# Decode attention and gated MLP on one core: two ring slots exchanged, x moved to the sync queue behind the q weights, the last W_down read cut into 5, 3 and 1 rows

## Chip, cores and metric

One core of a Trainium2 chip. The metric is the device time of one execution in microseconds (us), lower is better. Runs of one kernel mostly lie within 1 us of their median, single ones up to 1.6 us off. The profiled span is about 1.8 us shorter than the device time of the same run (381.1 for 382.86): it runs from the program's first instruction to its last.

Names used below, as in the profile of the kernel before: PE runs the matmuls (1629; PEld is the loading of their weights, 1629 too), DVE, ACT and POOL run the other operations (157, 95 and 38 instructions), and SP issues all loads but x. The loads run as packets on 16 DMA engines; 4224 of the 6390 packet records, with 87% of the bytes, are of 32 KB. A load's landing is the last update of its semaphore in the trace (16 updates for a 4 MB tile, 5 for x). The granted clock is the share of full speed that the profile gives for PE, in the mean 0.864 before.

## The reference

A batch of 4 tokens goes through a pre-norm attention over the last 4096 positions of a cache, then a pre-norm ReGLU MLP:

```python
# x: 4 x 1 x 576; K and V cache: 4 x 16 x 16384 x 128; W = 4096; 32 q heads on 16 kv heads
q = (layernorm(x) @ wq).reshape(...)                    # wq 576 x 4096
k, v = k_cache[:, :, -4096:], v_cache[:, :, -4096:]     # each kv head serves 2 q heads
o = softmax(q @ k.T * 128 ** -0.5) @ v
h = x + o @ wo                                          # wo 4096 x 576
g = layernorm(h) @ W_gate                               # 576 x 4608, W_up the same
out = h + (relu(g) * (layernorm(h) @ W_up)) @ W_down    # 4608 x 576
```

Nearly all of it is reading: 159.6 MB, of which K and V are 134 MB in 32 tiles of 4 MB (K0 to K15, V0 to V15).

## The kernel before

All large loads are issued from SP, one after the other. K and V tiles and the q weights go through a ring of four 4 MB slots; a load into a slot waits, on SP, until the last reader of the slot is done, and everything behind it in SP's program waits with it: K3, and K4 behind it, waited 36.2 us there for K0's matmuls.

```python
def add_kv(kind, g):                 # next ring slot; its earlier owner must be finished
    s = ring_slot()
    place((kind, g), off, TILE, ("QK", g, 1) if kind == "K" else ("PV", g), ...)
...
add_kv("K", 0)                                            # slot 3
s = ring_slot(); place(("wq", 0), ..., "QMM", ...)        # slot 0: first 512 rows of wq
P.dma("sync", ("L", "wq", 1), ... last_rows(A_wq) ...)    # last 64 rows of wq, outside the ring
for g in range(1, NTILE):                                 # K1 slot 1, K2 slot 2, K3 slot 3, K4 slot 0,
    add_kv("K", g)                                        # V0 slot 1, K5 slot 2, V1 slot 3, K6 slot 0 ...
    if g >= 4:
        add_kv("V", g - 4)
...                                                       # then wo, W_gate, W_up
for j in range(4):                                        # W_down, 4 chunks of 9 rows per partition
    for r0, r1 in ((0, 9),) if j < 3 else ((0, 6), (6, 9)):
        place(("wd", j, r0), ...)
```

x (4.5 KB) was issued from ACT. In DVE's program the norm of x stands ahead of K0's transposes, and q_keep, which K0's matmuls need, stands behind them. The traces show them in that order: K0 had landed at 13.29 us before, but the transposes started behind the norm, at 14.59, and q_keep as they ended, at 29.25:

```python
P.dma("scalar", ("L", "x"), ... x_bf ...)
dve("bn0"), dve("bn1"), ...      # norm of x, 3.4 us to its transposed copy xnT
pe_x(); dve_x()                  # xnT
turn_k(0, 0); turn_k(0, 1)       # DVE: K0's two transposes, 7.4 us each; they do not read x
pe_q()                           # PE: q = xn @ wq ("QMM"); K3's or K4's slot is free after it
act_q(); dve_q()                 # q_keep
put_q(0); put_q(1)               # ACT: q into the matmuls' weights; K0's matmuls ("QK", 0) wait for it
```

## Time and profile before

| | before |
|---|---|
| device time, median of the first 3 runs | 381.62 us |
| data read | 159.6 MB, mean 419 GB/s over the span |
| packets in flight from 3.0 to 372.8 us (packet records) | 16 for 92% of the time, under 14 for less than 0.1 us in all |
| one 4 MB tile, landing to landing | 9.7 us |
| last W_down piece lands / last matmul ends | 377.55 / 378.41 us |

The page of the profile before: the busy share of the 16 DMA engines and their throughput in 40 equal slices of 9.5 us, and the queue that SP issues on with its share of the engines' span.

```profile
DMA  8999999999999999999999999999999999999993
GB/s 331 440 423 421 406 440 437 433 428 427 420 439 440 424 433 426 433 430 435 433 430 427 435 430 423 435 433 433 430 428 433 427 439 430 423 435 427 419 414 123
...
q1 hardware_dynamic: 6352, 159.59, 97.7%
```

The reader sees a kernel bound by its loads from the second slice to the last but one.

The timeline of the kernel before, DVE, ACT and PE in the first 46 us, six of its rows. Columns: start, duration, engine and line, operation, what it writes and reads, count, and in brackets the idle time ahead of it and what ended that.

```profile
11.19 0.80 DVE L354 BATCH_NORM_STATS2 sb_bn<-sb_x_bf 4x6 f32<-4x288 bf16 x2
14.59 14.69 DVE L432 STREAM_TRANSPOSE sb_arena<-sb_arena 128x4096 f32<-128x4096 f32 x2
23.01 3.60 PE L388 MATMUL psb<-sb_arena,sb_xnT 128*32 128x512 bf16 x32 [8.88 <-DMA sb_arena<-in_A_wq_dram]
29.25 0.68 DVE L409 CAST sb_q_keep<-psb 32x512 bf16<-32x512 f32 x1
29.96 2.53 ACT L418 COPY sb_arena<-sb_q_keep 32x128 bf16<-32x128 bf16 x8 [1.37 <-DVE sb_q_keep L409]
31.35 15.18 PE L450 MATMUL psb<-sb_arena 128*128 128x512 bf16 x47 [2.14 <-ACT sb_arena L418]
```

K0's two transposes take 14.7 us and end at 29.28; K0's matmuls start 2 us after that. The q weights landed before: the first 512 rows at 23.0, the last 64 at 24.2. The first norm instruction at 11.19 stands on DVE behind one that waited 7.2 us for a constant that POOL makes; x had been there since 2.4.

The timeline of SP of the kernel before, from K1 to V2: when each load was issued. The row of four holds K1 to K4; K3 is its third, issued at 40.09. Then come V0, K5, V1, K6, V2, K7, V3.

```profile
2.51 38.77 SPq L246 DMA_DIRECT2D sb_arena<-in_A_k_cache_dram  x4
53.90 0.54 SPq L246 DMA_DIRECT2D sb_arena<-in_A_v_cache_dram  x1
64.27 0.53 SPq L246 DMA_DIRECT2D sb_arena<-in_A_k_cache_dram  x1
74.64 0.54 SPq L246 DMA_DIRECT2D sb_arena<-in_A_v_cache_dram  x1
88.36 0.54 SPq L246 DMA_DIRECT2D sb_arena<-in_A_k_cache_dram  x1
97.43 0.54 SPq L246 DMA_DIRECT2D sb_arena<-in_A_v_cache_dram  x1
```

Each issue came before the stream had used up what was ahead of it. From 53 to 79 us the loads took 19 to 20 us to land, half of it spent queueing behind another tile (three issues of the kernel before, view of one line):

```profile
DMA to landing us min/median/max: 19.0/19.7/20.3
```

That queue is the margin. Taken from the first packet of a load (1.3 us after its issue) to the end of the packets ahead of it, it is 1 to 3 us at K3 (issued 40.09, K2's packets end at 42.6 to 44.5), 6 to 7 us at V0, K5 and V1, and only about 2 us at K6, on the engine that is done first.

### The profile page before, as it was taken

To read this page: it belongs to the slowest core of one execution; us is meant where nothing else is said; L and a number is where in the kernel's file an instruction comes from. 1 tells how busy PE (TensorE), PEld (TensorE's weight loads), DVE (VectorE), ACT (ScalarE), POOL (GpSimd) and SP (SyncE) were. 2 spreads that over 40 slices of the span, in tenths; PEclk is the share of its full clock that TensorE was granted. 3 is DMA by queue.
4 is the path that set the end of the run, shared out by engine and by line. 5 is a ranking of instruction groups with operands and counts; after the bars stand their busy time and mean duration, and the time that the engine had idled before them with its cause. 6 is when DMAs were issued, how large, how long until landed. Compare 5 with 4: busy or idle time off the path is not lost.

```text
span 381.1 us, 3671 instructions
## 1 busy us (share of the span) xinstructions
PE 278.0 (73%) x1629; PEld 92.8 (24%) x1629; DVE 223.2 (59%) x157; ACT 37.5 (10%) x95; POOL 16.3 (4%) x38
## 2 busy tenths in 40 slices
PE   0057999989959892979996939899969537036544
PEld 0013223322222221222221212222212213015322
DVE  0796799979383917965828279756464455002210
ACT  1112000015000006000000051000000340000100
POOL 8800000000000000000000000000000000000000
PEclk9998999989978897798997887989989956756687
DMA  8999999999999999999999999999999999999993
GB/s 331 440 423 421 406 440 437 433 428 427 420 439 440 424 433 426 433 430 435 433 430 427 435 430 423 435 433 433 430 428 433 427 439 430 423 435 427 419 414 123
DMA packets 6390, 159.81 MB, mean 419 GB/s; under 512 B 740, under 2 KB 744, under 8 KB 1384
## 3 DMA queue, kind: packets, MB, share of 16 engines
q1 hardware_dynamic: 6352, 159.59, 97.7%
q8 instruction: 12, 0.20, 0.2%
q14 instruction: 2, 0.02, 0.0%
q10 hardware_dynamic: 24, 0.01, 0.0%
HBM read 159.58 MB, written 0.00 MB: 419 GB/s over the span
## 4 chain that ended last, share of the span: by engine, by line
PE 44%; DMA 34%; DVE 15%; POOL 2%; ACT 2%; issue 1%; SPq 0%; POOLq 0%
PE psb L450 38%; DMA sb_arena<-in_A_k_cache_dram 19%; DVE sb_arena L432 11%; DMA sb_arena<-in_B_W_down_dram 9%; DMA sb_arena<-in_A_v_cache_dram 7%; PE psb L497 5%; POOL sb_arena L303 2%; ACT sb_pp L475 2%; DVE sb_o_sel L509 1%; DVE sb_o_tmp L505 1%; DVE sb_pp L484 1%; PE psb L534 0%; ACT sb_arena L418 0%; SPq L286 0%; PE psb L469 0%
## 5 line engine op out<-in xcount | busy, mean ns | idle before, releaser
L450 PE MATMUL psb<-sb_arena 128*128 128x512 bf16 x512 | 209.1, 578 | 10.5 <-DVE sb_arena L432 8.2
L432 DVE STREAM_TRANSPOSE sb_arena<-sb_arena 128x4096 f32<-128x4096 f32 x32 | 156.1, 4901 | 48.5 <-DMA sb_arena<-in_A_k_cache_dram 48.4
L450 PEld LDWEIGHTS psb<-sb_arena 128*128 128x128 bf16 x512 | 56.8, 114 | 153.6 <-issue 130.3
L497 PE MATMUL psb<-sb_arena,sb_pp 128*32 128x512 bf16 x512 | 35.9, 431 | 23.0 <-DMA sb_arena<-in_A_v_cache_dram 16.5
L475 ACT ACTIVATE sb_pp<-psb,sb_stat 128x512 bf16<-128x512 f32 x32 | 24.9, 847 | 247.8 <-DVE sb_stat L470 247.8
L505 DVE TENSOR_TENSOR sb_o_tmp<-psb,sb_qm 128x512 f32<-128x512 f32 x16 | 10.8, 676 | 27.9 <-PE psb L497 27.9
L497 PEld LDWEIGHTS psb<-sb_arena,sb_pp 128*32 128x32 bf16 x512 | 13.6, 106 | 47.9 <-issue 22.7
L457 DVE TENSOR_REDUCE sb_stat<-psb 128x1 f32<-128x1024 f32 x4 | 4.8, 1211 | 24.2 <-PE psb L450 24.2
L484 DVE STREAM_TRANSPOSE sb_pp<-sb_pp 128x2048 bf16<-128x2048 bf16 x8 | 18.0, 2278 | 1.4 <-ACT sb_pp L475 1.4
L509 DVE TENSOR_REDUCE sb_o_sel<-sb_o_tmp 128x128 f32<-128x512 f32 x16 | 16.6, 1037 | 0.6
L534 PE MATMUL psb<-sb_o_sel,sb_selw 128*32 128x32 f32 x128 | 2.4, 232 | 16.3 <-DVE sb_o_sel L509 16.3
L668 PE MATMUL psb<-sb_arena,sb_hnT 128*32 128x384 bf16 x120 | 7.9, 437 | 6.6 <-DMA sb_arena<-in_B_W_up_dram 4.5
L375 PE MATMUL psb<-sb_ident_b,sb_xn_bf 4*128 4x4 bf16 x4 | 0.3, 172 | 13.7 <-DVE sb_xnd_bf L364 13.7
L388 PE MATMUL psb<-sb_arena,sb_xnT 128*32 128x512 bf16 x32 | 3.6, 631 | 8.9 <-DMA sb_arena<-in_A_wq_dram 8.9
L675 DVE TENSOR_TENSOR sb_pp<-psb,sb_pp 128x384 bf16<-128x384 f32 x3 | 1.5, 551 | 12.6 <-PE psb L668 12.6
L517 PE MATMUL psb<-sb_stat,sb_sameh 128*128 128x1 f32 x8 | 1.8, 292 | 9.1 <-DVE sb_stat L515 9.1
L303 POOL MEMSET sb_arena<- 128x8192 f32 x1 | 6.9, 6925 | 0.0
L475 ACT ACTIVATION_READ_ACCUMULATOR sb_pp<-psb,sb_stat 128x1 f32 x32 | 6.6, 208 | 0.0
L668 PEld LDWEIGHTS psb<-sb_arena,sb_hnT 128*32 128x32 bf16 x120 | 4.2, 124 | 9.7 <-DMA sb_arena<-in_B_W_up_dram 4.8
L534 PEld LDWEIGHTS psb<-sb_o_sel,sb_selw 128*32 128x32 f32 x128 | 1.9, 142 | 17.4 <-DVE sb_o_sel L509 17.4
L701 PE MATMUL psb<-sb_arena,sb_pp 128*32 128x144 bf16 x144 | 3.8, 250 | 3.0 <-DMA sb_arena<-in_B_W_down_dram 2.5
L418 ACT COPY sb_arena<-sb_q_keep 32x128 bf16<-32x128 bf16 x16 | 4.8, 303 | 1.5 <-DVE sb_q_keep L409 1.4
(123 smaller groups left out, 71.9 us busy)
## 6 DMA issues: line engine op xcount, KB each, us to landing
sb_arena<-in_A_k_cache_dram SPq DMA_DIRECT2D x16, 4096.0 KB, 18.9
sb_arena<-in_A_v_cache_dram SPq DMA_DIRECT2D x16, 4096.0 KB, 24.2
sb_arena<-in_A_wo_dram SPq DMA_DIRECT2D x1, 4608.0 KB, 16.0
sb_arena<-in_B_W_gate_dram SPq DMA_DIRECT2D x1, 4608.0 KB, 30.9
sb_arena<-in_B_W_up_dram SPq DMA_DIRECT2D x1, 4608.0 KB, 42.3
sb_arena<-in_A_wq_dram SPq DMA_DIRECT2D x1, 4096.0 KB, 21.5
sb_arena<-in_B_W_down_dram SPq DMA_DIRECT2D x3, 1296.0 KB, 31.1
sb_arena<-in_B_W_down_dram SPq DMA_DIRECT2D x1, 864.0 KB, 32.7
```

The lines of the kernel that those rows point to most:

```text
L303: pool("c_qW", lambda e: e.memset(arena[:, 0:2 * QWW].bitcast(FP32), 0.0))
L418: act(("QW", b), lambda e, i=i: e.copy(out=bass.AP(tensor=arena, offset=32 * i * AW + b % 2 * QWW + 32 * i, ap=[[AW, 32], [128, 4], [514, ...
L432: dve(("TRA", g, w), lambda e: e.transpose(out=dst, in_=src), [("L", "K", g)] if w == 0 else [])
L450: pe(("QK", g, w), lambda e, off=off, steps=steps, wo_=wo_, qd=qd, first=first, last=a == cb == 3: e.matmul(bank[SB[b % 2] + w], lhsT=aren ...
L457: dve(("MAX", b), lambda e: e.tensor_reduce(out=stat[:, b, 0:1], in_=s_ps, axis=AX.X, op=ALU.max, negate=True), [("QK", 4 * b + 3, 1)])
L475: act(("EXP", b, w), lambda e, w=w, a=a: e.activation(out=bass.AP(tensor=pp, offset=4096 + a // 2 * 2048 + w * 1024 + a % 2, ap=[[8192, 12 ...
L484: dve(("PTR", b, w), lambda e: e.transpose(out=dst, in_=src), [("EXP", b, w), ("PV", 4 * b - 1) if b else "QMM"])
L497: pe(("PV", g), lambda e, j=j, tq=tq, k=k: e.matmul(o_ps[32 * j:32 * j + 32, :], lhsT=pT[:, qd * 1024 + tq * 32:][:, 0:32], rhs=v[:, tq * ...
L505: dve(("OS", g), lambda e: e.tensor_tensor(out=o_tmp[:, :].rearrange("p (t d) -> p t d", t=4), in0=o_ps.rearrange("p (t d) -> p t d", t=4) ...
L509: dve(("OSEL", g), lambda e: e.tensor_reduce(out=o_sel[:, qd, :], in_=o_tmp[:, :].rearrange("p (t d) -> p d t", t=4), axis=AX.X, op=ALU.ad ...
L534: pe(("OT", b), lambda e, q=q, qd=qd: e.matmul(ot_ps[32 * qd:32 * qd + 32, 0:32], lhsT=selw[:, qd, 32 * q:32 * q + 32], rhs=o_sel[:, qd, 3 ...
L668: pe(("GU", g, c // 4), lambda e, g=g, m=m, j=j, lo=lo, c=c: e.matmul(bank[3 * g + m][32 * j:32 * j + 32, 0:384], lhsT=hnT[:, c if c < 4 e ...
```

## The change

Three edits, each aimed at one wait: K3 may be loaded as soon as the q weights are used; x gives up its queue of its own (q10 in the trace before, its four packets start at 1.85 to 2.03 us) and goes in line on SP; and fewer matmuls (4 instead of 12) are left when the last piece of W_down lands.

```diff
+        first = ring[0]
+        ring[0] = first + 1
         add_kv("K", 0)
+        ring[0] = first
         s = ring_slot()
 ...
         P.dma("sync", ("L", "wq", 1), ... last_rows(A_wq) ...)
+        P.dma("sync", ("L", "x"), ... x_bf ...)
+        ring[0] = first + 2
         for g in range(1, NTILE):
 ...
-            for r0, r1 in ((0, 9),) if j < 3 else ((0, 6), (6, 9)):
+            for r0, r1 in ((0, 9),) if j < 3 else ((0, 5), (5, 8), (8, 9)):
 ...
-        P.dma("scalar", ("L", "x"), ... x_bf ...)
 ...
-                    if n == 0 and (r == 0 or (j == 3 and r == 6)):
+                    if n == 0 and (r == 0 or (j == 3 and r in (5, 8))):
```

More of the change, by code (lines that the diff above doesn't have):

```diff
@@ L260, in bass_sequential_preLN__sliding_block_cached__glu_gated_reglu__decode_kernel @@
         P.dma("sync", ("L", "wq", 1), lambda e: e.dma_start(out=pT[:, 0:2048], in_=last_rows(A_wq)), "d_wq1")
+        P.dma("sync", ("L", "x"), lambda e: e.dma_start(out=x_bf[:, :], in_=A_x.rearrange("b s d -> (b s) d")), "d_x")
+        ring[0] = first + 2
         for g in range(1, NTILE):
@@ L351, in bass_sequential_preLN__sliding_block_cached__glu_gated_reglu__decode_kernel @@
         act("warm_sqrt", lambda e: e.activation(out=warm[:, 0:1], in_=eps_c[:, :], func=ACT.Sqrt), ["c_eps"])
-        P.dma("scalar", ("L", "x"), lambda e: e.dma_start(out=x_bf[:, :], in_=A_x.rearrange("b s d -> (b s) d")), "d_x")
         for hf in range(2):
```

## The prediction

> **What bounds it now.** The load stream. The DMA row of the 40 slices is 9 from slice 2 to 39; queue q1 takes 97.7% of 16 engines' span. In the packet records 14 to 16 packets are in flight from 3.0 to 372.8 us. A 4 MB tile takes 9.7 us (landings 54.8, 64.5, 74.2 us). The last W_down piece lands at 377.55, the last matmul ends at 378.45.
>
> **Slot exchange.** K3 reuses the slot of K0 or wq. Before, it waited for K0's matmuls and was issued at 40.09 us, while K2's packets ended at 42.6 to 44.5: no engine ran dry. After, K3 waits for the q matmuls (about 32 us) and K4 for K0's. Gain: none; it only widens a margin.
>
> **x move.** Today x rides on the ACT queue: its four packets run at 1.9 us, its last semaphore update is at 2.4. [...] So x behind K0, wq and wq's last rows lands when those do, about 24.2 us. The norm chain now starts at 11.19, held by a constant from POOL, so it starts 13 us later. DVE is in order and K0's transposes (2 x 7.42 us) stand behind it: they end at 42.3, not 29.3. The q copies add 2.1: K0's matmuls start at 44.4 (31.35 before), end at 53.1 (40.09).
>
> **How much is critical.** I step the early ring forward with the trace's durations (QK: K0 8.7, K1 13.8, K2 and K3 10.4 us; issue to first packet 1.2 to 1.4):
> - K4 issued 53.1, K3's packets end 52.7 to 54.4: gap 0 to 1.6 us
> - V0 issued 67.0, K4's end 64.0: gap about 4
> - K5 77.3, V1 87.7: gaps about 0.7
> - K6: K4's matmuls end at 99.0 (88.36 before); gap 1.7
> - V2 needs PV0, after a PE stall on K5's first transpose; a clock dip to 0.5, as after the stall at 80 us today, would cost 1.7 us: issued 109 to 111, gap 0.4 to 2
>
> After that PE needs about 16 us per K and V pair and DMA 19.4: DMA is saturated again, but lost stream time is never regained. V2's packets end at 120 to 122 us; before 111.0 on the fastest engine, 112.6 on the slowest. The slowest sets the end: loss 7.4 to 9.2 us.
>
> **Tail.** Matmuls behind the last landing fall from 12 to 4, about 20 ns each, and the 3-row piece lands only 0.34 us earlier (estimate, from 430 GB/s). Gain 0.2 to 0.4 us; the added small DMA costs about 0.1.
>
> **Predicted:** 381.6 + 8.5 - 0.3 = 389.8 us, range 386.8 to 392.3. Faster by over 2%: 1%; within 2%: 39%; slower by over 2%: 60%.
>
> **What would show it.** The first norm instruction near 24.2 us instead of 11.2; K0's matmuls near 44.4. K3's issue near 32, K4's near 53. GB/s below 400 in slices 6 to 11, then as before, shifted. PE from 44 to 95 us almost solid. Last landing to last matmul 0.6 us instead of 0.9.
>
> **What would make it wrong.** x landing well before the q weights: then neutral, about 381.3. A different clock in the early stage (each 3.4 us dip moves it 1.7). The slowest engine's lag (3.3 us at the end of W_down) shrinking after the gaps, worth 1 to 2 us. Wider gaps if K4 or K5 stall more.

The landing near 24.2 us is the author's estimate, and the trace of the kernel before supports it: SP's loads landed in the order of their issue (K0 13.29, wq 22.96, wq's last rows 24.24, K1 33.96).

Its other figures of the hardware, as the traces have them: first packets 1.41 us after issue at K0, 1.32 and 1.31 at K4 and V0 after the change; clock dips to 0.5 from 31.29 to 34.70 and from 82.49 to 85.90 us before, 3.41 us each, half of which is the 1.7; W_down's matmuls 18 to 21 ns each (72 in 1.31 us, 36 in 0.75 us, before); the added piece under 0.1 us (e4).

## The result, and the profile after

The changed kernel takes 392.38 us (391.6 to 392.64, 4 runs) against 381.69 us (4 runs) before. The ratio is 1.0275 (95% interval 1.0255 to 1.0294): slower by over 2%. Ratios here are the mean time of one kernel's runs over that of the other's of the same rounds, so not quite the ratio of the medians quoted.

The page of the profile after, the same two rows of slices (of 9.75 us):

```profile
DMA  7999986999999999999999999999999999999994
GB/s 323 430 431 434 435 316 269 397 410 375 377 414 429 434 435 429 431 434 430 429 434 430 437 429 430 430 429 430 430 432 434 430 430 434 419 443 416 438 402 179
```

The loss sits in slices 6 to 12, about 49 to 117 us. Afterwards the stream runs at 430 GB/s as before, only later.

The chain of waits that ended last, followed in order of time, of the kernel after. Columns: start, duration, what the time went to.

```profile
2.51 21.79 DMA sb_x_bf<-in_A_x_dram
24.30 0.02 issue
24.33 0.82 DVE sb_bn L358 x2
...
27.68 6.29 DVE sb_arena L436
33.97 0.90 issue
34.87 7.40 DVE sb_arena L436
42.27 0.52 DVE sb_q_keep L413
...
44.21 49.21 PE psb L454 x140
...
96.05 4.37 DVE sb_arena L436
100.46 7.06 PE psb L454 x16
107.52 1.84 PE psb L501 x32
109.36 7.01 PE psb L454 x16
116.38 0.02 issue
116.39 16.53 DMA sb_arena<-in_A_k_cache_dram
```

This is the whole story in one column. x takes 21.8 us from issue to landing (4.5 KB!), then the norm runs, then K0's transposes, then PE is busy without a break for 49 us, and only at 116.4 does the chain go back to a load. In the chain of the kernel before, PE's first long stretch ended at 64.3, and a load (K5) came next.

The timeline of SP after, from x on. The row of four is K1 to K4; K3 was issued at 32.19 and K4 at 53.72, then V0, K5, V1, K6, V2.

```profile
2.51 0.64 SPq L264 DMA_DIRECT2D sb_x_bf<-in_A_x_dram  x1
3.19 51.06 SPq L246 DMA_DIRECT2D sb_arena<-in_A_k_cache_dram  x4
67.53 0.54 SPq L246 DMA_DIRECT2D sb_arena<-in_A_v_cache_dram  x1
77.90 0.53 SPq L246 DMA_DIRECT2D sb_arena<-in_A_k_cache_dram  x1
88.27 0.54 SPq L246 DMA_DIRECT2D sb_arena<-in_A_v_cache_dram  x1
99.44 0.54 SPq L246 DMA_DIRECT2D sb_arena<-in_A_k_cache_dram  x1
109.41 0.53 SPq L246 DMA_DIRECT2D sb_arena<-in_A_v_cache_dram  x1
```

V0, K5 and V1 are issued 13.6 us later than before, more than the 6 to 7 us of margin. K6 and V2 are 11 and 12 us later. The three issues from 53 to 79 us (K4, V0, K5) of the kernel after:

```profile
DMA to landing us min/median/max: 12.3/12.3/12.4
```

They no longer queue behind a whole tile. In the packet records the 16 engines stand idle for 2.4 us on average before K4, 3.7 before V0 and 0.1 before K5, whose first packets start just as V0's last ones end. A tile lands 12.3 us after its issue, but the next is issued 10.4 to 13.8 us after it (53.72, 67.53, 77.90, 88.27). The successive landings of K4, V0, K5, V1, K6, V2 and K7 come 11.7, 13.8, 10.4, 11.7, 10.6, 9.9 and 10.3 us after the one before, together 10.7 us more than seven times 9.7.

The packet records of this stage say what these microseconds are. From 43 to 124 us the engines stood idle for 7.6 us on average, and the 32 KB packets took 3.2 us per engine more than 1.21 us each would have; in e6, which lost nothing (see the experiments), it is 0.0 and 0.5. The difference, 7.6 and 2.7, is about the 10.1 us by which K7 lands later than in e6 (122.81).

### The profile page after: what moved, and what is told of

Same layout as the page of the kernel before. It is cut to its first block, busy times and chain, and to the rows that moved or that the text cites. A ratio compares the mean times of both kernels' runs of the same rounds, so it can differ in the third digit from the quotient of the medians.

```text
span 389.8 us, 3672 instructions
## 1 busy us (share of the span) xinstructions
PE 277.4 (71%) x1629; PEld 92.2 (24%) x1629; DVE 223.0 (57%) x157; ACT 37.6 (10%) x95; POOL 16.0 (4%) x38
## 4 chain that ended last, share of the span: by engine, by line
PE 48%; DMA 33%; DVE 14%; ACT 2%; SPq 1%; issue 1%
PE psb L454 42%; DMA sb_arena<-in_A_k_cache_dram 13%; DVE sb_arena L436 10%; DMA sb_arena<-in_B_W_down_dram 8%; DMA sb_arena<-in_A_v_cache_dram 6%; DMA sb_x_bf<-in_A_x_dram 6%; PE psb L501 5%; ACT sb_pp L479 2%; DVE sb_o_sel L513 1%; DVE sb_o_tmp L509 1%; DVE sb_pp L488 1%; SPq L291 1%; PE psb L473 0%; PE psb L538 0%; ACT sb_arena L422 0%
## 5 line engine op out<-in xcount | busy, mean ns | idle before, releaser
L454 PE MATMUL psb<-sb_arena 128*128 128x512 bf16 x512 | 208.7, 577 | 20.3 <-ACT sb_arena L422 10.3
L501 PE MATMUL psb<-sb_arena,sb_pp 128*32 128x512 bf16 x512 | 36.4, 436 | 21.8 <-DMA sb_arena<-in_A_v_cache_dram 15.4
L509 DVE TENSOR_TENSOR sb_o_tmp<-psb,sb_qm 128x512 f32<-128x512 f32 x16 | 10.8, 676 | 26.5 <-PE psb L501 26.5
L501 PEld LDWEIGHTS psb<-sb_arena,sb_pp 128*32 128x32 bf16 x512 | 13.8, 107 | 47.1 <-issue 23.2
L672 PE MATMUL psb<-sb_arena,sb_hnT 128*32 128x384 bf16 x120 | 9.3, 498 | 6.2 <-DMA sb_arena<-in_B_W_up_dram 4.0
L679 DVE TENSOR_TENSOR sb_pp<-psb,sb_pp 128x384 bf16<-128x384 f32 x3 | 1.5, 551 | 13.6 <-PE psb L672 13.6
L358 DVE BATCH_NORM_STATS2 sb_bn<-sb_x_bf 4x6 f32<-4x288 bf16 x2 | 0.8, 439 | 12.9 <-DMA sb_x_bf<-in_A_x_dram 12.9
L672 PEld LDWEIGHTS psb<-sb_arena,sb_hnT 128*32 128x32 bf16 x120 | 4.7, 139 | 10.5 <-DMA sb_arena<-in_B_W_up_dram 4.7
## 6 DMA issues: line engine op xcount, KB each, us to landing
sb_arena<-in_B_W_down_dram SPq DMA_DIRECT2D x1, 720.0 KB, 31.9
```

The source lines that it names most:

```text
L454: pe(("QK", g, w), lambda e, off=off, steps=steps, wo_=wo_, qd=qd, first=first, last=a == cb == 3: e.matmul(bank[SB[b % 2] + w], lhsT=aren ...
L501: pe(("PV", g), lambda e, j=j, tq=tq, k=k: e.matmul(o_ps[32 * j:32 * j + 32, :], lhsT=pT[:, qd * 1024 + tq * 32:][:, 0:32], rhs=v[:, tq * ...
L509: dve(("OS", g), lambda e: e.tensor_tensor(out=o_tmp[:, :].rearrange("p (t d) -> p t d", t=4), in0=o_ps.rearrange("p (t d) -> p t d", t=4) ...
L672: pe(("GU", g, c // 4), lambda e, g=g, m=m, j=j, lo=lo, c=c: e.matmul(bank[3 * g + m][32 * j:32 * j + 32, 0:384], lhsT=hnT[:, c if c < 4 e ...
```

## The experiments

The theory: x, now behind 9 MB in SP's queue, lands at 24.3 instead of 2.4 us. The norm of x is late, and K0's transposes, behind it in DVE's program, are late with it (27.59 instead of 14.59). PE starts 13 us late and frees slots 11 to 14 us late. The ring takes up some of it and the stream runs empty for the rest. The rivals: (A) the slot exchange costs, since K4 now waits for K0's matmuls; (B) the extra small piece of W_down costs; (C) a DMA of four rows on SP's queue costs in itself, wherever it stands.

| kernel | median us | ratio to before (95%) | K0's matmuls start, us |
|---|---|---|---|
| the change | 392.38 | 1.0275 (1.0255 to 1.0294) | 44.2 |
| e1: change, x back on ACT | 381.87 | 1.0009 (0.9990 to 1.0029) | 31.4 |
| e2: before, x moved only | 394.49 | 1.0331 (1.0315 to 1.0348) | 44.1 |
| e3: before, slots exchanged only | 381.81 | 1.0004 (0.9991 to 1.0017) | 31.4 |
| e4: before, pieces only | 382.03 | 1.0010 (0.9997 to 1.0024) | 31.3 |
| e5: change, x first on SP | 381.96 | 1.0007 (0.9994 to 1.0019) | 31.9 |
| e6: change, x behind K0 on SP | 381.28 | 0.9992 (0.9979 to 1.0006) | 33.2 |
| e7: change, K0's transposes ahead of the norm | 386.93 | 1.0138 (1.0121 to 1.0155) | 39.2 |
| e8: change, half of them ahead | 385.70 | 1.0102 (1.0081 to 1.0123) | 36.9 |
| e9: before, six drains forced | 401.71 | 1.0511 (1.0495 to 1.0526) | 31.4 |

All nine gave the right result. e1 to e4, e5 to e7 and e8 to e9 ran in three groups, each group on one chip and beside its own runs of the kernel before (medians 381.52, 381.62, 381.71).

### e1: the change with x back on the ACT queue

```diff
-        P.dma("sync", ("L", "x"), ...)
+        P.dma("scalar", ("L", "x"), ...)      # where it stood before
```

> The change with x back on the ACT queue; slot exchange and 5/3/1 pieces stay. Theory (late x holds DVE, K0's transposes and so every slot release): 381.0 to 381.7 us, a ratio to before of 0.998 to 1.001, K0's matmuls start near 31.3 us, no tile landing more than 10.5 us after the last until W_O. Rival A (the exchange makes the loads wait): stays near 392. Rival B (the extra small piece costs at the end): stays near 392 too.

381.87 us, ratio 1.0009: a little over the expected range, but within the interval the same as before. The loss is gone though exchange and pieces are still there. So A and B, as causes of the loss, are out. One detail missed: between two landings up to 10.9 us passed, not 10.5; the kernel before has 11.0 as well (see e9 for what falls into such tiles).

### e2: the kernel before with x moved and nothing else

```diff
         P.dma("sync", ("L", "wq", 1), ...)
+        P.dma("sync", ("L", "x"), ...)
 ...
-        P.dma("scalar", ("L", "x"), ...)
```

> The kernel before with nothing changed but x on the sync queue behind the q weights. Theory: K3 and K4 are both issued near 53.7 us, one gap of some 12 us in the load stream between K2's and K3's packets, then no further gap until K6; K6 lands near 113.6 (112.7 in the full change). Total 392 to 394 us: at most 1.5 us slower than the full change. If the exchange is what costs (rival A): about 381.5. If the exchange rescues a lot once x is late: 396 or more.

394.49 us, ratio 1.0331. The move alone makes all of the loss and a little more. The time is 0.5 us over the expected range, and K6 landed at 115.1 instead of 113.6: V1 landed 10.8 us after K5, without any gap in the stream. Where the loss went is another picture than in the change: K3 waits for K0's matmuls, is issued at 53.1 and lands 21.8 us after K2; then the next three tiles follow at 9.7 us, since K4 was issued right behind it. Two stretches of this kernel (columns: the stretch and its length; busy us and count of PE, PEld, DVE, ACT and POOL; granted clock of PE, DMA share, GB/s):

```profile
44.00:55.00 11.00, 10.85 (x37) 4.04 (x38) 11.00 (x3) 1.23 (x5) 0.00 (x0) 0.82 0.14 37
55.00:67.00 12.00, 12.00 (x29) 3.17 (x28) 10.38 (x3) 0.00 (x0) 0.00 (x0) 1.00 0.94 407
```

and of the full change, four stretches:

```profile
55.00:67.00 12.00, 12.00 (x29) 3.17 (x28) 12.00 (x3) 0.00 (x0) 0.00 (x0) 1.00 0.87 350
67.00:80.00 13.00, 13.00 (x40) 4.03 (x39) 13.00 (x4) 0.00 (x0) 0.00 (x0) 1.00 0.89 358
80.00:91.00 11.00, 11.00 (x35) 3.46 (x33) 8.23 (x2) 0.00 (x0) 0.00 (x0) 1.00 0.94 387
91.00:102.00 11.00, 9.95 (x34) 3.08 (x33) 6.63 (x5) 5.92 (x15) 0.00 (x0) 1.00 0.93 383
```

One hole of 11 us in e2 (engines idle for 11.5 us on average from 43 to 124 us, slow packets 0.7), a string of smaller ones in the change (7.6 and 3.2), the same late PE behind both. The exchange, worth nothing when x is early (e3), saves about 2 us when x is late (ratio 1.0331 against 1.0275, different groups), a bit more than the 1.5 us that I had allowed.

### e3: the slot exchange alone

```diff
+        first = ring[0]
+        ring[0] = first + 1
         add_kv("K", 0)
+        ring[0] = first
 ...
+        ring[0] = first + 2
         for g in range(1, NTILE):
```

> The kernel before with the slot exchange alone. Theory: neutral, 381.2 to 382.0 us, ratio within 0.2% of 1; K3 issued near 27.5 us, K4 near 40. Rival A (the exchange costs by letting K4 wait on K0): 385 or more.

381.81 us, ratio 1.0004. K3 was issued at 27.6 us instead of 40.1 and landed at 54.8 us, as before. Neutral, as expected: the load waited in the queue instead of on SP.

### e4: the pieces of 5, 3 and 1 rows alone

```diff
-            for r0, r1 in ((0, 9),) if j < 3 else ((0, 6), (6, 9)):
+            for r0, r1 in ((0, 9),) if j < 3 else ((0, 5), (5, 8), (8, 9)):
```

> The kernel before with the last W_down chunk in pieces of 5, 3 and 1 rows. Theory: 381.3 to 381.7 us, 0 to 0.4 us faster; last landing to last matmul falls from 0.9 to about 0.6 us. Rival B (the extra piece costs): slower by over 1 us.

382.03 us, ratio 1.0010, the interval holds 1: no gain, and no loss of over 1 us. Beside e3, whose third W_down chunk landed at the same 373.35, the last landing to the end of the last matmul fell from 0.60 us (376.45 to 377.05) to 0.36 us (376.72 to 377.07), but the last landing itself came 0.27 us later. Not all of that is the extra piece: on the engine that is done first the last chunk takes 3.16 to 3.19 us in the seven kernels with three pieces and 3.10 to 3.12 in the four with two, so the piece costs under 0.1 us; the rest is one late engine. A gain of 0.2 us is too small to be told apart in these traces.

### e5 and e6: x on SP's queue, but earlier in it

```diff
+        P.dma("sync", ("L", "x"), ...)          # e5: here, as SP's first load
         first = ring[0]
         ring[0] = first + 1
         add_kv("K", 0)
+        P.dma("sync", ("L", "x"), ...)          # e6: here instead
         ring[0] = first
 ...
-        P.dma("sync", ("L", "x"), ...)          # both: no longer behind wq
```

> The change with x on the sync queue but as its first load, ahead of K0. Theory (only the time at which x lands matters): 381.2 to 382.3 us, x lands near 2.5 us, all later loads up to 0.7 us later since their issue stands behind x's. Rival C (a small DMA of 4 rows on the sync queue costs in itself[...]): near 392.

381.96 us, ratio 1.0007. K0 landed at 13.8 instead of 13.3 us. Rival C is out: x as the first load on SP's queue cost nothing that shows (1.0007), x behind wq on the same queue did (1.0275).

> The change with x on the sync queue between K0 and the q weights. Theory: x lands near 13.3 us, the norm chain starts there, 2 us later than before and 11 us earlier than in the change; K0's matmuls start near 33.4; the ring's margin takes up the 2 us: 381.3 to 382.3 us. If the loss goes with the delay of x one to one: 383.4 or more.

381.28 us, ratio 0.9992. The norm chain and PE started 2 us later than before, and nothing came of it. The timeline of e6:

```profile
13.17 0.81 DVE L358 BATCH_NORM_STATS2 sb_bn<-sb_x_bf 4x6 f32<-4x288 bf16 x2 [1.79 <-DMA sb_x_bf<-in_A_x_dram]
16.62 14.67 DVE L436 STREAM_TRANSPOSE sb_arena<-sb_arena 128x4096 f32<-128x4096 f32 x2
33.23 17.36 PE L454 MATMUL psb<-sb_arena 128*128 128x512 bf16 x50 [3.97 <-ACT sb_arena L422]
```

So the loss does not go with the delay of x one to one: the ring absorbs 2 us entirely and 13 us only in part.

### e7 and e8: x late, but K0's transposes not behind it

```diff
+        for w in range(2):                      # e7; range(1) in e8
+            dve(("TRA", 0, w), ...)             # K0's transposes, in front of the norm chain
         for hf in range(2):
             dve(f"bn{hf}", ...)
 ...
-        turn_k(0, 0)
-        turn_k(0, 1)                            # stays in e8
```

> The change, x still late on the sync queue, but K0's two transposes stand ahead of the norm chain on DVE. Theory (in-order DVE with the 14.7 us of transposes behind x): the transposes run 13.3 to 28.1 us, the norm chain 28.1 to 31.4, K0's matmuls start near 39.9 instead of 44.2, K4 is issued near 49.3; gain 3 to 6 us on the change, 386.5 to 389.5 us. If the order on DVE doesn't matter (the q weights or something else holds K0's matmuls): 392.

386.93 us, ratio 1.0138. x is as late as in the change, yet half of the loss is gone. The timeline of e7:

```profile
13.13 14.68 DVE L359 STREAM_TRANSPOSE sb_arena<-sb_arena 128x4096 f32<-128x4096 f32 x2 [1.75 <-DMA sb_arena<-in_A_k_cache_dram]
27.66 0.74 DVE L363 BATCH_NORM_STATS2 sb_bn<-sb_x_bf 4x6 f32<-4x288 bf16 x2
37.19 0.68 DVE L418 CAST sb_q_keep<-psb 32x512 bf16<-32x512 f32 x1 [6.25 <-PE psb L403]
39.20 11.37 PE L459 MATMUL psb<-sb_arena 128*128 128x512 bf16 x38 [2.05 <-ACT sb_arena L427]
```

This shows the middle link of the theory: what x held up was the 14.7 us of transposes standing behind it on DVE, which never read x.

> The change, x still late, but the first half of K0's transpose stands ahead of the norm chain on DVE and the second half behind it. Theory: the chain still starts near 24.3 us, the second half ends near 35.0, K0's matmuls start near 37.1 (44.2 in the change, 39 to 40 in e7); only the gaps at K6 and V2 remain; 382.5 to 385.0 us. If the loss follows the start of K0's matmuls one to one: 387 or more.

385.70 us, ratio 1.0102: K0's matmuls start at 36.9 as stepped, but the time is 0.7 us above the expected range. V1, K6, V2 and K7 landed 11.2, 11.0, 9.9 and 10.0 us after the tile ahead of them, although K6 and V2 were the only loads I had expected to be late, and by little. From 43 to 124 us the engines were idle for only 1.1 us on average, but the 32 KB packets took 2.6 us per engine more than 1.21 us each (0.5 in e6): of the 4.0 us that are left of the loss, slow packets make more than idle engines do. That is the term that e9 measures.

### e9: what one drain costs

The same in the middle of the stream, with nothing late: V5 to V10 are each issued only when the load ahead has landed.

```diff
+            after = [("L", "K", g + 4)] if kind == "V" and 5 <= g <= 10 else []
+            place((kind, g), ..., key=f"slot{s}", extra=after)     # extra: more to wait for
```

> The kernel before with six loads (V5 to V10) each issued only when the load ahead of it has landed, so that the stream runs empty six times in its saturated part, nothing else changed. Measures what one restart costs. Theory now (a gap costs the idle time and some 0.7 us more, as the first packets after it take about 1.9 us instead of 1.21): about 0.35 to landing, 0.1 to issue, 1.3 to the first packet and 0.7 more, 2.3 to 2.6 us each, 395 to 397.5 us in all. If a restart costs the idle time alone, as predicted: 1.75 us each, 391 to 393 us.

401.71 us, ratio 1.0511: 3.3 us for each drain, more than either theory. The view of the one line, one of the six loads (V7):

```profile
L247 SPq DMA_DIRECT2D sb_arena<-in_A_v_cache_dram x1: 535/535/535, 207.4 to 207.4; - x1
...
DMA to landing us min/median/max: 12.4/12.4/12.4
```

The six took 12.4 to 12.5 us from issue to landing and were issued 0.02 us after the landing ahead of them; so each cost 12.4 - 9.7 = 2.7 us. In the packet records the first packets of such a tile start 1.3 us after its issue. In the six tiles, 4 to 14 of the 16 engines begin at 1.3 to 1.6 us and take 1.7 to 2.1 us for their first 32 KB, and the others begin at 1.9 us or later; in the running stream 32 KB take 1.21 us. The rest of the 3.3 us is one late engine: of the K tiles that follow the six (K10 to K15), four landed 10.9 to 11.5 us after their forerunner, with fifteen engines done 1.2 to 1.7 us before the sixteenth. Where the stream runs on, engines that are done go ahead with the next tile: before, K2's packets end at 42.6 to 44.5 us, and 15 or more packets are in flight throughout. In e9 V6 to V10 are issued only after K10 to K14 have landed, so there all engines wait for the last.

The packet records also show what falls into these four tiles. Queue q8 carries 12 or 13 instruction packets of 16 KB in each kernel, about 1 us each. While one runs in a full stream, 15 engines instead of 16 have a load packet; so it is in all eleven traces. In e9 such packets start at 179.74, 221.82, 253.06 and 295.17 us, one in each of K10, K12, K13 and K15, the four late tiles, and none in K11 and K14, which landed on time. This is a match of times in traces; no run moved these packets.

## Why the prediction was right, and where it was short

Right in direction and mechanism, point by point:

- **x's landing.** Predicted 24.2, measured 24.30; its four packets started at 23.43 to 23.71 us, and the norm started at 24.33. The last rows of wq, just ahead of x in SP's program, end between 23.2 and 23.9, so x came in line behind them.
- **The chain.** K0's matmuls at 44.4 predicted, 44.21 measured; e6, e7 and e8 moved that point to 33.2, 39.2 and 36.9, and the time went with it, but not one to one.
- **The gates.** K4, V0, K5, V1, K6, V2 predicted at 53.1, 67.0, 77.3, 87.7, 99.0 and 109 to 111; measured 53.7, 67.5, 77.9, 88.3, 99.4 and 109.4. The half us is K0's matmuls, 9.5 us instead of 8.7: TensorE's granted clock was 0.5 from 35.5 to 49.1 us, and PE had stood idle from 33.9 to 44.2; at half clock it ran 4.9 us of K0's matmuls, against 3.4 us before (31.3 to 34.7). The dip that I allowed for around 100 us did not come (1.0 from 49.1 to 120.8).
- **The slot exchange.** Neutral by itself (e3), as said. That it softens a late x by 2 us I had not said.

The size was short: 8.2 us predicted, 10.5 measured (1.0275 of 381.7). The median of 392.38 lies at the upper end of the range, 0.1 beyond it. Three terms of the sum were off:

1. **"issue to first packet 1.2 to 1.4", and then 9.7 us for the tile.** The first part holds (1.3 from the start of SP's issuing instruction, 0.8 from its end). But a tile that finds the engines empty lands 12.3 us after its issue, where 1.3 + 9.7 + 0.35 (last packet to landing) makes 11.35. About 1 us per cold tile was missing, as e2 (12.3), e9 (12.4 to 12.5) and the change itself show. The gaps themselves were sized well (7.6 us of idle engines, for a loss of 7.4 to 9.2 forecast from gaps); the slow packets behind them, 2.7 us more than in e6, have no term in the prediction. The two aren't independent, since a tile that lands late shortens the idle time ahead of the next (V0 landed 13.8 us after K4, and ahead of K5 only 0.1 us is idle). V2, the last gated load, was issued as predicted (109.41), but its packets, slow as well, began up to 2.4 us after the issue, when K6's ended, and it landed 13.2 us after it.
2. **The slowest engine as the reference.** I took 112.6 us for V2 and the 3.3 us of lag at the end from one profile. That run took 382.86 us, 1.2 us over the median, and K7 landed 10.9 us after V2; in e3, e4, e5 and e6 it came 9.7 to 9.8 us after. Against that profile the last landing moved by 9.3 us (377.55 to 386.81), against e6's by 10.1 (376.68). The lag did not come from a fixed slow engine that the holes would have absorbed; it varies from run to run, and in the change V1, K6 and V2 took 13.2 to 13.8 us to land: an instruction packet (94.05 us, 0.94 us long) falls into V1, where one engine pauses from 94.06 to 94.98, and K6 and V2 start behind the late engines of the tile ahead.
3. **"Gain 0.2 to 0.4 us"** at the tail is not there (e4): the wait for the last matmuls fell by 0.24 us, but the last landing came 0.27 us later. The extra piece is under 0.1 of that, as I had put it; the rest is a late engine and not the edit, so this term is not settled.

How the missing 2.3 us divide among the three can't be told exactly from single profiles. What remains open is why a cold tile's first packets are slow, and whether the instruction packets make one engine late: in e9 they fall into just the late tiles, but no run moved them.

No version here beats the kernel before: e1, e3, e5 and e6 equal it. The stream is full from 3 to 373 us in it, and none of the three edits shortens the stream.

## What to carry to other kernels

Here a load's place in its queue decided when it landed, not its size: 4.5 KB behind 9 MB took 21.8 us (1.5 us on a queue of its own: issued at 0.91, landed at 2.40). So what DVE read first had to be loaded first, and work that did not need it had to stand ahead of it (e7: 386.93 instead of 392.38 us). In this ring, which kept the stream full, a delay cost only what exceeded the margin at each slot (2 us cost nothing in e6), so step the ring forward gate by gate (this placed six issues within 0.6 us), and charge a restart with the measured cold time of a tile (12.3 us here), not with the running one (9.7). An edit that let a load be issued earlier gained nothing while the queue ahead of it was never empty (e3: K3 issued 12.5 us earlier, ratio 1.0004).
